# Rows turned by VectorE from 32-feature pieces, and one 512-column matmul for both parts of w2, in a two-layer mixture-of-experts kernel

## The chip, the cores and the metric

The kernel runs on one core of one Trainium2 chip. The metric is the device time of one execution in microseconds (us); lower is better. The median of three runs before the change is 2756.77 us (2755.84 to 2760.04).

## The reference

A Fourier transform over a batch of 8 x 3072 tokens of 256 features is followed by two mixture-of-experts layers, each with 8 experts of 256 -> 1024 -> 256 and one expert per token (top 1). Cut to what matters:

```python
def _attn_ref(x):                       # x: (8, 3072, 256)
    X = np.fft.fft(x, axis=1)
    X = np.fft.fft(X, axis=2)
    return X.real.astype(np.float32)

def _moe_ref(x, w_gate, w1, w2):        # x: (24576, 256)
    logits = x @ w_gate
    ...                                 # softmax, argmax
    for e in range(E):
        mask = expert_idx == e
        xe = x[mask]
        h = np.maximum(xe @ w1[e], 0.0)
        ye = h @ w2[e]
        out[mask] = gate_w[mask, None] * ye
```

The second layer (`_moe2_ref`) computes its logits from normalised rows and expert embeddings, and its experts in the same way.

## The kernel before, in words

The transform comes first (`fft`). Each of its rows is routed to an expert and scattered by GpSimd into a DRAM buffer `scr1`, grouped by expert: 256 features, the token's number and its gate, 258 floats a row (`ROWW`). Then follow two loops with the same code (`Layer.loop`): the first reads blocks of 256 rows (`T`) from `scr1`, computes the first layer's experts, routes again and scatters into `scr2`; the second reads `scr2` and scatters the results into `out`. Each loop runs some 99 steps, one block a step.

Precision: every factor of a matmul is split into a high and a low part in float32r, and the products high x high, high x low and low x high are summed in PSUM. So `x` becomes `xh` and `xl`, the hidden values `hh` and `hl`, the weights `w1h`, `w1l`, `w2h`, `w2l`.

A step `s` in the order in which it is written (and so stands in each engine's queue; `tc.manual_schedule()` keeps the written order):

- SyncE loads the block of step s + 2 (`load_rows`, L1179, one transfer into `xrow`; the first two blocks of a layer come earlier by `ahead`, L1186 and L1191), and, where the expert changes, the next weights into `stage` (L1042 to L1061). A step whose expert doesn't change skips those by a condition.
- `epilogue(s - 1)` begins: ScalarE evicts the accumulator `y` of the block before, times the gate, into `yrow` (`take`, L1273); in the first loop VectorE takes the eight logits (L1288), in the second the token numbers (L1278).
- `layer1`, four groups of 12 matmuls of 256 columns (L1243), each evicted by ScalarE (`hh`, relu, L1246) and VectorE (`hl`, relu and subtraction, L1247).
- `transpose` of the block s + 1 (L1228): TensorE turns the four 128 x 128 pieces into one PSUM bank `aux`, ScalarE casts `xh` (L1232), VectorE subtracts `xl` (L1233). `xh` and `xl` exist once, so this stands behind the step's first layer.
- the splitting of new weights, and in the first loop the routing on VectorE.
- `layer2` (L1255): 16 times (8 pieces of the hidden dimension, 2 halves of the block) three matmuls, hh x w2h, hh x w2l and hl x w2h, into `y[:, tb, :w2]`. In the first loop a row has 264 columns (256 and the 8 logits of the next router), in the second 256. `y` has one PSUM bank of 512 floats for each half.
- in the first loop TensorE counts ranks (L145, L148) from the one-hot `ohm` (L127); then GpSimd scatters (L178).

## Time and profile before

| | |
|---|---|
| median of 3 runs | 2756.77 us (2755.84 to 2760.04) |
| the profiled execution: time | 2754.11 us |
| the profiled execution: span of its instructions | 2752.2 us |
| TensorE matmul busy | 97% |
| VectorE, ScalarE, GpSimd busy | 47%, 39%, 29% |
| transform and routing ahead of the first loop | about the first 360 us |
| first loop, second loop | to about 1575 us, and from about 1600 to 2735 us |

A matmul's record runs from its start to the modelled end of its pipeline; the next one starts long before that end. So matmuls are priced by the distance from start to start, which the timeline gives, and the busy share says only that something was always under way.

### The profile page before, as it was taken

The numbers are of one execution on the slowest core, as the hardware profiler recorded it, in microseconds if no ns is written. First come the engines' busy times: TensorE is split into PE (matmuls) and PEld (weight loads), VectorE is DVE, ScalarE is ACT, GpSimd is POOL, SyncE is SP. The second block draws the span as 40 slices with busy tenths as digits, with TensorE's granted clock in tenths as the row PEclk, the third lists the DMA queues.
The fourth block names the chain that finished last, engine by engine and source line by source line (L and its number), as shares of the span: only waits on it lengthen the run. The fifth ranks groups of instructions, "written<-read, shape, count | busy, mean of one in ns | idle before, by whom it ended". The sixth has DMA issues, their size and how long they took to land. (4 is left out here: it accounts for less than half of the span.)

```text
span 2752.2 us, 66450 instructions
## 1 busy us (share of the span) xinstructions
PE 2659.2 (97%) x21695; PEld 2569.8 (93%) x21695; DVE 1306.1 (47%) x3870; ACT 1062.8 (39%) x2456; POOL 789.0 (29%) x875
## 2 busy tenths in 40 slices
PE   7888799999999999999999899999999999999998
PEld 4566689999999999999999899999999999999997
DVE  5776545556555665557555632343323323343232
ACT  2444434444444454445444433343333333343332
POOL 4877712233222332224222321111111111111111
PEclk9998899999999999999999999999999999999999
DMA  8677411122111331113111211131112211131121
GB/s 257 205 233 230 163 43 41 48 82 83 45 48 40 117 112 43 48 52 110 47 43 53 74 54 44 50 102 47 48 47 78 76 45 44 47 108 47 63 61 39
DMA packets 152349, 221.43 MB, mean 80 GB/s; under 512 B 40982, under 2 KB 120383, under 8 KB 151946
## 3 DMA queue, kind: packets, MB, share of 16 engines
q1 hardware_dynamic: 117658, 122.37, 16.3%
q0 software_dynamic: 31984, 94.02, 9.6%
q8 instruction: 180, 2.95, 0.5%
q14 instruction: 223, 1.83, 0.2%
q10 hardware_dynamic: 2304, 0.26, 0.1%
HBM read 529.18 MB, written 82.24 MB: 222 GB/s over the span
## 5 line engine op out<-in xcount | busy, mean ns | idle before, releaser
L1247 DVE SCALAR_TENSOR_TENSOR hl<-ph,hh 128x512 fp32r<-128x512 f32 x793 | 546.0, 691 | 904.2 <-ACT hh L1246 903.9
L1255 PE MATMUL py<-w2h,hh 128*128 128x264 f32 (+1 forms) x3184 | 918.1, 288 | 1.1 <-DVE lgm L1288 0.6
L1243 PE MATMUL ph<-xh,w1h 128*128 128x256 f32 x3172 | 900.4, 284 | 8.5 <-PEq L1485 5.5
L1255 PE MATMUL py<-w2h,hl 128*128 128x264 f32 (+1 forms) x3184 | 901.3, 283 | 0.1
L1255 PE MATMUL py<-w2l,hh 128*128 128x264 f32 (+1 forms) x3184 | 901.2, 283 | 0.2 <-DVE w2l L1097 0.2
L1243 PE MATMUL ph<-xh,w1l 128*128 128x256 f32 x3172 | 891.1, 281 | 0.0
L1243 PE MATMUL ph<-xl,w1h 128*128 128x256 f32 x3172 | 890.8, 281 | 0.1
L1246 ACT ACTIVATE hh<-ph 128x512 fp32r<-128x512 f32 x793 | 472.2, 599 | 574.6 <-PE ph L1243 562.1
L1243 PEld LDWEIGHTS ph<-xh,w1h 128*128 128x128 f32 x3172 | 599.5, 189 | 9.3 <-ACTq L1219 5.7
L1255 PEld LDWEIGHTS py<-w2h,hh 128*128 128x128 f32 x3184 | 601.4, 189 | 1.6 <-ACT hh L1246 1.5
L1255 PEld LDWEIGHTS py<-w2h,hl 128*128 128x128 f32 x3184 | 600.9, 189 | 0.9 <-DVE hl L1247 0.9
L1255 PEld LDWEIGHTS py<-w2l,hh 128*128 128x128 f32 x3184 | 601.4, 189 | 0.4 <-DVE w2l L1097 0.4
L1243 PEld LDWEIGHTS ph<-xh,w1l 128*128 128x128 f32 x3172 | 600.0, 189 | 0.0
L1243 PEld LDWEIGHTS ph<-xl,w1h 128*128 128x128 f32 x3172 | 599.6, 189 | 0.4 <-DVE xl L1233 0.4
L178 POOL DMA_INDIRECT out<-yrow,idx x194 | 188.7, 973 | 948.6 <-ACT yrow L1273 886.8
L1273 ACT ACTIVATE yrow<-py,xrow 128x256 f32<-128x256 f32 x368 | 154.4, 471 | 603.1 <-PE py L1255 431.9
L178 POOL DMA_INDIRECT scr<-yrow,pos x196 | 205.0, 1046 | 457.2 <-DVE lgm L1288 300.6
L178 POOL DMA_INDIRECT scr<-row,pos x192 | 208.0, 1084 | 69.8 <-issue 45.3
L1302 POOL TENSOR_TENSOR ssm<-ssm,half 128x2 f32<-128x2 f32 x98 | 75.1, 766 | 402.5 <-ACT sq L1299 379.4
L1233 DVE TENSOR_TENSOR xl<-aux,xh 128x512 fp32r<-128x512 f32 x201 | 136.9, 681 | 13.7 <-ACT xh L1232 7.7
L1232 ACT CAST xh<-aux 128x512 fp32r<-128x512 f32 x201 | 117.1, 582 | 18.2 <-PE aux L1228 18.2
L1228 PE MATMUL aux<-ident,xrow 128*128 128x128 f32 x736 | 110.3, 272 | 0.1
(276 smaller groups left out, 1925.1 us busy)
## 6 DMA issues: line engine op xcount, KB each, us to landing
stage<-in_moe_w SPq DMA_DIRECT2D x305, 1024.0 KB
stage<-in_moe_w SPq DMA_DIRECT2D x206, 512.0 KB
xrow<-scr SPq DMA_DIRECT2D x184, 258.0 KB
stage<-in_x SPq DMA_DIRECT2D x16, 768.0 KB
lw<-in_moe_w SPq DMA_DIRECT2D x8, 1024.0 KB
scr<-zrow SPq DMA_DIRECT2D x16, 258.0 KB
stage<-ext SPq DMA_DIRECT2D x102, 32.0 KB
scr<-yrow,pos POOLq DMA_INDIRECT x196, 3.3
```

The costliest lines, as they stand in the source:

```text
L178: ins = k.nc.gpsimd.indirect_dma_start(out=dst, out_offset=bass.IndirectOffsetOnAxis(ap=idx, axis=0), in_=src, in_offset=None, bounds_chec ...
L1228: nc.tensor.transpose(ps[:, dd * T + tb * P : dd * T + tb * P + P], t[:, tb, dd * P : dd * P + P], self.k.ident)
L1232: nc.scalar.copy(m.xh, pv)
L1233: self.v.tensor_tensor(m.xl, pv, m.xh, ALU.subtract)
L1243: nc.tensor.matmul(ps[:, f], lhsT=wa[i][:, dd, fs], rhs=xa[:, dd], start=n == 0, stop=n == 5)
L1246: nc.scalar.activation(m.hh[:, hs], ps, AF.Relu)
L1247: self.v.scalar_tensor_tensor(m.hl[:, hs], ps, 0.0, m.hh[:, hs], ALU.max, ALU.subtract)
L1255: self.nc.tensor.matmul(m.y[:, tb, : self.w2], lhsT=ha[:, f, ts_], rhs=wa[i][:, f, : self.w2], start=f == 0 and n == 0, stop=f == 7 and n ...
L1273: nc.scalar.activation(yr[:, tb, :D], y[:, tb, :D], AF.Copy, scale=tag[:, tb, 1:2])
L1302: nc.gpsimd.tensor_tensor(ss, ss, k.half, ALU.pow)
```

## The change

1. A block no longer comes as rows. `Rows` holds a tile `x` of 128 x 8 x 2 x 32 and a small tile `tag` with the token's number and gate. `fetch` loads `x` by four transfers, one for each quarter of the partitions, in pieces of 32 features (128 bytes), and `tag` by one.
2. `turn`, one VectorE instruction, transposes 32 x 32 blocks of `x` into `xt` (128 features x 2 x 256 tokens, SBUF). In the loops it stands between the beginning of the epilogue and the first layer. `parts` makes `xh` and `xl` from `xt` where `transpose` stood. The transposes on TensorE go.
3. The high and low parts of w2 lie beside each other in one tile (`w2hl`). In the second loop `layer2` makes one matmul of 512 columns, hh x (w2h | w2l), and one of 256 for hl x w2h. The two halves of the accumulator are added by VectorE in the epilogue, with the gate, onto `yrow`.
4. The pool `lt` (turned pieces of w2 ahead of the first loop) has three buffers instead of four.

```diff
+class Rows:
+    def __init__(self, pool, name, bufs=(1, 1)):
+        self.x = pool.tile([P, 8, 2, 32], F32, name=name + "x", bufs=bufs[0])
+        self.tag = pool.tile([P, 2, 2], F32, name=name + "t", bufs=bufs[1])
...
-    lo.wp = ctx.enter_context(tc.tile_pool(name="lt", bufs=4, side="right"))
+    lo.wp = ctx.enter_context(tc.tile_pool(name="lt", bufs=3, side="right"))
...
+            w = pool.tile([P, 8, 2, w2], F32R, name=f"w2{len(self.w2hl)}")
+            self.w2hl.append(w)
+            self.w2h.append(w[:, :, 0])
+            self.w2l.append(w[:, :, 1])
...
-            t = self.m.xr.tile([P, 2, ROWW], F32, name="xrow") if s < self.nlive else self.m.xe[s - self.nlive]
+            t = Rows(self.m.xr, "xrow", (4, 5)) if s < self.nlive else self.m.xe[s - self.nlive]
         r = self.reg(s, 0, 0, self.k.bound + 1 - T)
-        self.nc.sync.dma_start(t, self.src[ds(r, T)].rearrange("(a p) w -> p a w", p=P))
+        self.fetch(t, self.src[ds(r, T)])
         return t
+
+    def fetch(self, t, rows, tag=True, **kw):
+        v = rows[:, :D].rearrange("(j b) (a q i) -> q j b a i", b=8, a=2, q=4)
+        out = [self.nc.sync.dma_start(t.x[32 * q : 32 * q + 32], v[q], **kw) for q in range(4)]
+        if tag:
+            out.append(self.nc.sync.dma_start(t.tag, rows[:, D:ROWW].rearrange("(a p) w -> p a w", p=P), **kw))
+        return out
...
         for i in range(2):
-            ins = self.nc.sync.dma_start(
-                self.m.row[i], self.src[i * T : i * T + T].rearrange("(a p) w -> p a w", p=P), cond=(c != 0)
-            )
+            for ins in self.fetch(self.m.row[i], self.src[i * T : i * T + T], cond=(c != 0)):
...
-            self.nc.sync.dma_start(self.m.row[0][:, :, :D], other.rearrange("(a p) w -> p a w", p=P), cond=(c == 0))
+            self.fetch(self.m.row[0], other, False, cond=(c == 0))
...
+    def turn(self, t):
+        self.v.transpose(self.m.xt.rearrange("p a (j b) -> p b a j", b=8), t.x)
+
+    def parts(self):
+        m = self.m
+        self.nc.scalar.copy(m.xh, m.xt)
+        self.v.tensor_tensor(m.xl, m.xt, m.xh, ALU.subtract)
+
     def transpose(self, t):
-        nc, m = self.nc, self.m
-        ps = self.k.ps_aux.tile([P, 512], F32, name="aux")
-        for dd in range(2):
-            for tb in range(2):
-                nc.tensor.transpose(
-                    ps[:, dd * T + tb * P : dd * T + tb * P + P], t[:, tb, dd * P : dd * P + P], self.k.ident
-                )
-        pv = ps.rearrange("p (d t) -> p d t", d=2)
-        nc.scalar.copy(m.xh, pv)
-        self.v.tensor_tensor(m.xl, pv, m.xh, ALU.subtract)
+        self.turn(t)
+        self.parts()
...
+                first, last = f == 0, f == 7
+                if self.first:
...
+                else:
+                    nc.tensor.matmul(m.y[:, tb], lhsT=m.hh[:, f, ts_], rhs=m.w2hl[i][:, f, :, :D], start=first, stop=False)
+                    nc.tensor.matmul(m.y[:, tb, :D], lhsT=m.hl[:, f, ts_], rhs=m.w2h[i][:, f, :D], start=False, stop=last)
...
         if not self.first:
             take()
+            for tb in range(2):
+                v.scalar_tensor_tensor(yr[:, tb, :D], y[:, tb, D:], tag[:, tb, 1:2], yr[:, tb, :D], ALU.mult, ALU.add)
...
-            ep = self.epilogue(rows[s - 1][:, :, 256:258], s - 1)
+            ep = self.epilogue(rows[s - 1].tag, s - 1)
             next(ep)
...
+            if s + 1 < ns:
+                self.turn(rows[s + 1])
             for g in range(4):
                 self.layer1(s, g)
             if s + 1 < ns:
-                self.transpose(rows[s + 1])
+                self.parts()
```

Where the instructions stand is shown by three places. On TensorE, in a step of the second loop, from the last matmuls of the first layer to the first of the second, before:

```order
L1243 MATMUL ph<-xl,w1h_4421 128x256
L1243 MATMUL ph<-xh,w1l_4422 128x256
L1228 MATMUL aux<-ident,xrow 128x128 x4
L1255 MATMUL py<-w2h_4423,hh 128x256
L1255 MATMUL py<-w2l_4424,hh 128x256
L1255 MATMUL py<-w2h_4423,hl 128x256
```

and in the changed kernel (where w_4417 is the tile with both parts of w2):

```order
L1263 MATMUL ph<-xl,w1h_3426 128x256
L1263 MATMUL ph<-xh,w1l_3427 128x256
L1286 MATMUL py<-w_4417,hh 128x512
L1287 MATMUL py<-w_4417,hl 128x256
L1286 MATMUL py<-w_4417,hh 128x512
```

The four transposes are gone, and of three matmuls of 256 columns two have become one of 512.

On VectorE, in a step of the second loop, before (idx is the cast of the token numbers):

```order
L1278 CAST idx<-xrow 128x2
L1247 SCALAR_TENSOR_TENSOR hl<-ph,hh 128x512 x4
L1233 TENSOR_TENSOR xl<-aux,xh 128x512
L1172 TENSOR_LOAD bchange
L1219 COMPARE_AND_BRANCH
```

and in the changed kernel:

```order
L1304 SCALAR_TENSOR_TENSOR yrow<-py,xrowt,yrow 128x256 x2
L1306 CAST idx<-xrowt 128x2
L1244 STREAM_TRANSPOSE xt<-xrowx 128x8x64
L1267 SCALAR_TENSOR_TENSOR hl<-ph,hh 128x512 x4
L1249 TENSOR_TENSOR xl<-xt,xh 128x512
L1186 TENSOR_LOAD bchange
```

The two sums and the turn of the next block now stand ahead of the four `hl`; in the first loop it is the turn alone, behind the logits.

On SyncE, a row load of the second loop with the register loads around it, before:

```order
L1169 TENSOR_LOAD brow
L1169 ISA x2
L1179 ISA
L1179 DMA xrow<-scr_58 128x2x258
L1169 TENSOR_LOAD bchange
```

and in the changed kernel (each ISA row prepares the transfer behind it):

```order
L1198 ISA
L1198 DMA xrowx<-scr_58 32x16x32
L1198 ISA
L1198 DMA xrowx<-scr_58 32x16x32
L1198 ISA
L1198 DMA xrowx<-scr_58 32x16x32
L1200 ISA
L1200 DMA xrowt<-scr_58 128x2x2
L1183 TENSOR_LOAD bchange
```

One transfer has become five (the first of the four stands just above these rows), ahead of the conditional weight loads of the step.

## Rows read from the trace of the kernel before

**Rows 1.** The page: busy us by engine, and the clock in 40 slices

```profile
PE 2659.2 (97%) x21695; PEld 2569.8 (93%) x21695; DVE 1306.1 (47%) x3870; ACT 1062.8 (39%) x2456; POOL 789.0 (29%) x875
PEclk9998899999999999999999999999999999999999
```

**Rows 2.** Windows, first and second loop: stretch, length, busy by engine, clock, DMA share

```profile
360.00:1575.00 1215.00, 1201.21 (x10135) 1192.47 (x10134) 688.47 (x2501) 519.03 (x1232) 336.98 (x415) 0.99 0.22 63
1600.00:2735.00 1135.00, 1135.00 (x9664) 1135.00 (x9664) 375.12 (x610) 387.88 (x711) 188.69 (x194) 1.00 0.19 60
```

**Rows 3.** Timeline of TensorE, second loop: start, duration (us), line, operation

```profile
2004.81 0.28 PE L1243 MATMUL ph<-xh,w1l 128*128 128x256 f32 x1
...
2005.49 0.28 PE L1255 MATMUL py<-w2l,hh 128*128 128x256 f32 x1
...
2010.89 0.28 PE L1255 MATMUL py<-w2h,hl 128*128 128x256 f32 x1
2011.01 0.28 PE L1243 MATMUL ph<-xh,w1h 128*128 128x256 f32 x1
...
2016.55 0.28 PE L1243 MATMUL ph<-xh,w1l 128*128 128x256 f32 x1
2016.67 0.60 PE L1228 MATMUL aux<-ident,xrow 128*128 128x128 f32 x4
2017.02 0.36 PE L1255 MATMUL py<-w2h,hh 128*128 128x256 f32 x1
2017.22 0.28 PE L1255 MATMUL py<-w2l,hh 128*128 128x256 f32 x1
```

**Rows 4.** Line L1228 (count, ns min/median/max), and one group by form

```profile
L1228 PE MATMUL aux<-ident,xrow x736: 270/273/299, 386.1 to 2685.8; 128*128 128x128 f32 x184
L1228 PE MATMUL aux<-ident,row x48: 270/273/445, 314.1 to 2709.3; 128*128 128x128 f32 x48
L1228 PE MATMUL aux<-ident,xe x20: 271/273/273, 1530.0 to 2732.7; 128*128 128x128 f32 x20
...
L1255 PE MATMUL py<-w2l,hh 128*128 128x256 f32 x1584 | 444.9, 281 | 0.0
```

**Rows 5.** Timeline of the weight loads, ahead of the first loop

```profile
353.11 0.97 PEld L371 LDWEIGHTS aux<-en,wt 128*128 128x128 f32 x8
```

**Rows 6.** Timeline of VectorE, ScalarE and TensorE: a step of each loop

```profile
1016.42 0.17 DVE L1288 TENSOR_TENSOR lgm<-py,xrow 128x16 f32<-128x16 f32 x1 [0.63 <-DVEq L1214]
1017.09 0.69 DVE L1247 SCALAR_TENSOR_TENSOR hl<-ph,hh 128x512 fp32r<-128x512 f32 x1 [0.50 <-ACT hh L1246]
...
1020.89 0.37 PE L1255 MATMUL py<-w2h,hh 128*128 128x264 f32 x1
...
1023.89 0.17 DVE L127 TENSOR_TENSOR ohm<-eq,mx 128x16 f16<-128x16 f32 x1
...
1026.82 0.19 PE L145 MATMUL aux<-ohm,tri 128*128 128x24 f16 x1
...
2011.21 0.84 ACT L1273 ACTIVATE yrow<-py,xrow 128x256 f32<-128x256 f32 x2 [5.01 <-PE py L1255]
...
2013.26 0.69 DVE L1247 SCALAR_TENSOR_TENSOR hl<-ph,hh 128x512 fp32r<-128x512 f32 x1 [5.09 <-ACT hh L1246]
```

**Rows 7.** Groups by form: the weights' low part on VectorE

```profile
L1081 DVE TENSOR_TENSOR w1l<-stage,w1h 128x1024 fp32r<-128x1024 f32 x36 | 47.2, 1344 | 17.6 <-ACT w1h L1080 14.6 <-issue 1.7 <-DVEq L1214 1.2
```

**Rows 8.** DMA queues (packets, MB, share of 16 engines), and two issues on SyncE

```profile
q1 hardware_dynamic: 117658, 122.37, 16.3%
...
q10 hardware_dynamic: 2304, 0.26, 0.1%
...
44.51 12.41 SPq L485 DMA_DIRECT2D col<-in_x  x16
...
2009.81 0.38 SPq L1179 DMA_DIRECT2D xrow<-scr  x1
```

**Rows 9.** Timeline ahead of the first step (SyncE), and at the end (GpSimd)

```profile
310.74 1.12 SPq L1186 DMA_DIRECT2D row<-scr  x2
...
2741.29 0.97 POOL L178 DMA_INDIRECT out<-yf,idxf  x1 [11.31 <-ACT yf L1273]
```

More of the change, by code (lines that the diff above doesn't have):

```diff
@@ L1009, in __init__ @@
         self.k = k
-        self.w1h, self.w1l, self.w2h, self.w2l = [], [], [], []
+        self.w1h, self.w1l, self.w2hl, self.w2h, self.w2l = [], [], [], [], []
         self.st, self.st2, self.stx = zip(*(self.views(k, i) for i in range(2)))
     def add_set(self, pool, w2, parts=(1, 2)):
-        for part in parts:
-            hs, ls, shape = ((self.w1h, self.w1l, [P, 2, F]), (self.w2h, self.w2l, [P, 8, w2]))[part - 1]
-            for ws, n in ((hs, "h"), (ls, "l")):
-                ws.append(pool.tile(shape, F32R, name=f"w{part}{n}{len(ws)}"))
+        if 1 in parts:
+            for ws, n in ((self.w1h, "h"), (self.w1l, "l")):
+                ws.append(pool.tile([P, 2, F], F32R, name=f"w1{n}{len(ws)}"))
+        if 2 in parts:
+            w = pool.tile([P, 8, 2, w2], F32R, name=f"w2{len(self.w2hl)}")
+            self.w2hl.append(w)
+            self.w2h.append(w[:, :, 0])
+            self.w2l.append(w[:, :, 1])
     @staticmethod
@@ L1120, in open_rows @@
         self.xl = wp.tile([P, 2, T], F32R, name="xl")
-        self.row = [wp.tile([P, 2, ROWW], F32, name=f"row{i}") for i in range(4)]
+        self.xt = wp.tile([P, 2, T], F32, name="xt")
+        self.row = [Rows(wp, f"row{i}") for i in range(4)]
     def open_front(self, ctx):
@@ L1142, in open @@
         self.xr = ctx.enter_context(tc.tile_pool(name="mx", bufs=5))
-        self.xe = self.row[2:] + [wp.tile([P, 2, ROWW], F32, name=f"xe{i}") for i in range(E - 3)]
+        self.xe = self.row[2:] + [Rows(wp, f"xe{i}") for i in range(E - 3)]
         self.yp = ctx.enter_context(tc.tile_pool(name="my", bufs=3))
@@ L1159, in __init__ @@
         self.sets = m.sets
-        self.w2 = D + E if m.first else D
         self.nlive = self.k.nb * S // T
@@ L1185, in ahead @@
         for i in range(2):
[L1186 to L1189 removed]
+            for ins in self.fetch(self.m.row[i], self.src[i * T : i * T + T], cond=(c != 0)):
+                self.k.tc.add_to_no_dep_group("sc1" if self.first else "sc2", ins.ins if hasattr(ins, "ins") else ins)
         if other is not None:
[L1191 removed]
+            self.fetch(self.m.row[0], other, False, cond=(c == 0))
     def stage1(self, s):
@@ L1253, in layer2 @@
                 ts_ = slice(tb * P, tb * P + P)
-                for n, (ha, wa) in enumerate(((m.hh, m.w2h), (m.hh, m.w2l), (m.hl, m.w2h))):
-                    self.nc.tensor.matmul(
-                        m.y[:, tb, : self.w2],
-                        lhsT=ha[:, f, ts_],
-                        rhs=wa[i][:, f, : self.w2],
-                        start=f == 0 and n == 0,
-                        stop=f == 7 and n == 2,
-                    )
+                first, last = f == 0, f == 7
+                if self.first:
+                    for n, (ha, wa) in enumerate(((m.hh, m.w2h), (m.hh, m.w2l), (m.hl, m.w2h))):
+                        nc.tensor.matmul(
+                            m.y[:, tb, : D + E],
+                            lhsT=ha[:, f, ts_],
+                            rhs=wa[i][:, f, : D + E],
+                            start=first and n == 0,
+                            stop=last and n == 2,
+                        )
+                else:
+                    nc.tensor.matmul(m.y[:, tb], lhsT=m.hh[:, f, ts_], rhs=m.w2hl[i][:, f, :, :D], start=first, stop=False)
+                    nc.tensor.matmul(m.y[:, tb, :D], lhsT=m.hl[:, f, ts_], rhs=m.w2h[i][:, f, :D], start=False, stop=last)
     def epilogue(self, tag, s, edge=False):
@@ L1322, in early @@
             if s:
-                ep = self.epilogue(row[0][:, :, 256:258], 0, True)
+                ep = self.epilogue(row[0].tag, 0, True)
                 next(ep)
@@ L1356, in late @@
             if s == 0:
-                ep = self.epilogue(row[0][:, :, 256:258], 0, True)
+                ep = self.epilogue(row[0].tag, 0, True)
                 next(ep)
@@ L1384, in loop @@
                 Layer.ahead(self.after)
-            ep = self.epilogue(rows[s - 1][:, :, 256:258], s - 1)
+            ep = self.epilogue(rows[s - 1].tag, s - 1)
             next(ep)
             if s >= nlive - 1:
-                nc.scalar.copy(m.cur, rows[s][:, :, 256:258])
+                nc.scalar.copy(m.cur, rows[s].tag)
+            if s + 1 < ns:
+                self.turn(rows[s + 1])
             for g in range(4):
```

3 lines of the change are left out of this document (1 added, 2 removed).

## The prediction, made blind

> **What bounds the kernel now.** I read the page's busy times first: TensorE is busy 2659.2 of 2752.2 us and holds the upper clock level (2.4 GHz) in nearly all slices [rows 1]. A share over the whole span says little, so next came the stretches: TensorE is busy 1201.21 of 1215 us in the first loop and 1135.00 of 1135 us in the second, while VectorE is busy 57% and 33%, and the DMA engines 22% and 19% [rows 2]. So in both loops TensorE's instruction stream sets the time, and the reader is to see what one step of it is made of.
>
> The timeline of one step of the second loop shows that [rows 3]. A busy time of 0.28 us for one matmul is not its price: the next starts 0.117 us later. From 2005.49 to 2010.89 lie 46 starts, so 5.40 / 46 = 0.1174 us. Going from the second layer's matmuls to the first layer's costs nothing extra (2010.89 to 2011.01). Going the other way, four transposes stand between, and there lies 2016.55 to 2017.22 = 0.67 us where two plain spacings would be 0.235 us: the four transposes and the slow first matmul behind them cost **0.44 us a step**. A step is 2016.55 - 2004.81 = 11.74 us (the same place one step earlier [rows 3]), so this is 3.7% of it.
>
> **The change, part by part.** *Transposes leave TensorE.* There are 736 + 48 + 20 = 804 of them [rows 4], 201 groups of four; each saves 0.44 us where TensorE runs without idling: 201 x 0.44 = 88 us. That holds only if what takes their place is hidden.
>
> *VectorE turns the rows.* No row shows such an instruction. It moves 512 columns from SBUF to SBUF; the nearest row is the weights' remainder, 1,024 columns SBUF to SBUF in 1.344 us [rows 7], so I take half, 0.67 us, with ends 0.5 (no fixed part) and 1.34 (each element passes twice). It stands ahead of the four hl instructions of its step. First loop: lgm ends at 1016.59, hl starts at 1017.09 because it waits for ScalarE [rows 6]; the turn fills that gap and delays the first hl by 0.2 to 0.85 us, to an end of 1018.6 at most. TensorE wants it at 1020.89. The later hl's each wait some 0.7 us for ScalarE, so the delay is gone by the second or third, and the one-hot ohm behind them (1023.89, wanted by TensorE at 1026.82) stays. Cost: 0, hidden behind the first layer's 5.6 us of matmuls.
>
> *The sum on VectorE in the second loop.* Two instructions of 256 columns; the same operation of 512 columns takes 0.69 us [rows 6], so at most 0.69 each. They wait for ScalarE's two evictions (2011.21 + 0.84 = 2012.05 [rows 6]). Queued behind them: the cast, the turn, the hl's. At the upper ends: 2012.05 + 1.4 + 0.2 + 1.34 = 2015.0, first hl done by 2015.7 instead of 2013.95; TensorE wants it at about 2017. Cost 0, with 1.3 us in hand. The accumulator y is read out by 2013.5, before it is written again at 2017. GpSimd's scatter waits about 1 us longer, and nothing waits for that but the end of the program.
>
> *xh and xl* read SBUF instead of PSUM, at the same place behind the last matmul of the first layer; some 5 us of second layer cover them. I take 0.
>
> *Row loads.* One transfer of 256 pieces becomes four of 512 pieces of 128 bytes and one of 256 pieces of 8. SyncE: sixteen transfers of 128 x 6 single floats, 768 pieces each, were issued in 12.41 us [rows 8], 0.78 us each or 1.0 ns a piece, so 2,304 pieces are about 2.3 us of issue for 0.38 now. Moved past that are only the weight loads of later steps, in a queue that waits for VectorE anyway. On the engines the nearest row by size is q10: 2,304 packets of 113 bytes on average in 0.1% of 16 x 2752 us, 19 ns each (10 to 29 by rounding); the other end is q1, 1,040 bytes on average, 16.3% over 117,658 packets, 61 ns [rows 8]. A row load is then 2304 x 19 / 16 = 2.7 us of every engine (8.8 at 61 ns). The load issued at 2009.81 [rows 8] belongs to the block that is turned at the start of the step after next, about 2024.7: 15 us of lead against 2.3 + 2.7 (11.1 at the upper end). Hidden.
>
> The Trainium skill speaks against this part ("DMA: Bandwidth & Descriptors", Specifications: transfers want pieces of at least 512 bytes for full rate, below that the engines read, modify and write). The trace agrees in bytes: 113 bytes in 19 ns is a third of the rate of 1,040 in 61. It changes the sum only if the row loads become the bound, which is the third rival.
>
> *One matmul of 512 columns for two of 256.* There are 1,584 such pairs [rows 4]. Two now cost 0.235 us. The one cannot be below 512 columns / 2.4 GHz = 0.213 us, and not above 0.235, since the same columns pass with one weight load less: a saving of 0 to 22 ns a pair, 0 to 34 us. What decides is whether the 0.117 - 0.107 = 10.7 ns that a 256-column matmul takes beyond its columns come per instruction or per column. Eight weight loads beside 8-column matmuls span 0.97 us, (0.97 - 0.19) / 7 = 0.111 us each [rows 5]: weights alone come nearly as slowly as the matmuls do, so the surplus looks tied to the load, one per instruction. I take 10.7 ns saved: 1584 x 0.0107 = **17 us**.
>
> By the Trainium skill ("TensorE: Matmul & The Clock Gate", Back-to-back issue gap) a matmul costs its columns plus about 2.5 ns. No row of the two loops agrees, 256 columns take 10.7 more; yet where 512 columns hide the load, that page's 0.216 us would save 19 ns a pair, 30 us, which is the first rival.
>
> *The ends.* Ahead of the first step SyncE issues two row loads in 1.12 us [rows 9]; now ten transfers and four more, and the turn of the first block stands in VectorE's queue ahead of weights and logits: 0 to 8 us once, and a little again between the layers; I take 4. At the end the sum adds at most 1.4 us ahead of the last scatter (2741.29 [rows 9]): 1. The smaller buffer count of the pool lt I price at 0: its next writer stands behind its last reader in TensorE's order already.
>
> **Sum**, against the profiled execution's own 2754.1 us (its span of 2752.2 and 1.9 around it): 2754.1 - 88 - 17 + 5 = 2654. The median of the three runs is 2.7 us above that execution, so 2657.
>
> **Rivals.** *First: a 512-column matmul at the bare column rate* (no surplus, since the load is long done): 30 to 34 us in place of 17, so 2640 to 2644. For it speaks the 0.111 us weight load; against it, that it needs the surplus to vanish whole.
>
> *Second: the surplus goes with the columns* (reading the moving operand is a little slower than the clock). Then the merge saves nothing and only the transposes count: 2757 - 88 + 5 = 2674. Nothing in the rows excludes it, since all matmuls of the loops have about one width.
>
> *Third, on the other side: the small pieces make the DMA engines the bound.* A step then lasts as long as its transfers: about 20% of 11.74 us are taken already, 2.3 us, and 144 pieces an engine come on top. From (11.74 - 2.3) / 144 = 66 ns a piece the step is longer than today, and the turn in VectorE's queue holds hl and with it TensorE. At 75 ns: 13.1 us a step, 1.4 x 198 steps = 277 us more, about 3030. For it: unaligned 128-byte reads from HBM beside weights, which no row shows; against it: q10's 10 to 29 ns, and col's pieces went by at 16 x 1.0 = 16 ns an engine.
>
> *Fourth: VectorE late in part.* If the turn costs 3 to 5 us, the first hl in the first loop comes after 1020.89, and ohm late: 0.4 us or more of 100 steps returns, 2700 to 2760. Against it: no row of 512 columns is above 0.7 us.
>
> That the transposes don't really go can be left aside: they are gone from TensorE's order.
>
> **How the numbers follow.** Forecast 2657: 0.55. First rival 0.16, second 0.16, third 0.07, fourth 0.06. The unknown ends (0 to 10 us) widen the three lower cases to 2636 to 2685; that holds 0.87, and the range ends there. A difference of 0.2% (5.5 us) is about what a measurement of this kernel can tell from no change. The first three cases are all faster, 0.87, and of the fourth I count 0.02 faster, 0.03 the same and 0.01 slower; with the third rival that makes 0.89, 0.03 and 0.08.
>
> **What would show it.** The matmuls of the two loops keep a spacing of 0.117 us, and a step of the second loop falls from 11.74 to 11.74 - 0.44 - 16 x 0.0107 = 11.13 us, of the first by 0.44. The 512-column matmul's start to the next start reads 0.213 to 0.235: that settles the first two rivals. VectorE's wait at the turn should be on y's eviction or nothing, not on a DMA; if a DMA ends it, the third rival is at work. The first hl should come by 2 us after where it is now at most, with no wait of TensorE for hl. The prediction is wrong if TensorE idles in the loops, or if the spacing of the 256-column matmuls grows because VectorE and the transfers now move more through SBUF.

## The result, and the profile after

The changed kernel takes 2698.28 us (median of four runs, 2691.82 to 2700.54), the kernel before, run beside it, 2758.4 us (2755.84 to 2760.32): a ratio of 0.9779, with an interval of 0.9765 to 0.9794. So it is faster, as forecast, but by 60 us where the forecast had 100, and it lies outside the range of 2636 to 2685. On a second chip the same two kernels gave 2699.54 and 2759.36 us, 0.9785 (0.9767 to 0.9804).

The page of the changed kernel (busy time by engine, the clock in 40 slices, the queue that carries the row loads) answers to [rows 1] and [rows 8], two of its windows (stretch, length, busy by engine, clock, DMA share) to [rows 2]:

```profile
PE 2574.2 (95%) x19307; PEld 2411.2 (89%) x19307; DVE 1575.5 (58%) x4269; ACT 1069.6 (40%) x2456; POOL 791.9 (29%) x875
...
PEclk9898789999999999999999999999999999999999
...
q1 hardware_dynamic: 546394, 122.42, 23.4%
```

```profile
400.00:1480.00 1080.00, 1067.37 (x8968) 1059.59 (x8967) 721.75 (x2399) 477.32 (x1123) 309.21 (x382) 0.99 0.30 65
1560.00:2680.00 1120.00, 1114.13 (x7901) 1041.27 (x7902) 559.62 (x961) 403.14 (x735) 198.96 (x202) 1.00 0.28 61
```

TensorE still has work in nearly all of both loops, and the DMA engines rose from 0.22 and 0.19 to 0.30 and 0.28 of their time without becoming the bound. What the windows hide is seen only when the steps are lined up one by one. The table is worked out from the start of the first matmul of each step (L1243 before, L1263 after), span against span:

| stretch | before, us | after, us | difference | the forecast's |
|---|---|---|---|---|
| start of the program to the first step | 315.4 | 327.4 | +12.0 | +4 |
| the first four steps | 78.1 | 82.1 | +4.0 | -1.8 |
| 87 steps of the first loop with no change of weights | 1054.6 | 1016.2 | -38.4 | -38.3 |
| the 7 steps that bring in an expert's new weights | 90.1 | 106.1 | +15.9 | -3.1 |
| step 94 of the first loop | 12.1 | 13.3 | +1.2 | -0.4 |
| the 4 steps between the loops | 61.8 | 58.9 | -2.9 | -2 |
| the 95 remaining steps of the second loop | 1114.7 | 1068.8 | -45.9 | -58.1 |
| behind the last step's start | 25.4 | 25.1 | -0.3 | +1 |
| span | 2752.2 | 2697.8 | -54.4 | -99 |

Three lines are wrong: the ends (with the first four steps, some 14 us), the weight-change steps (19 us, and 1.6 us in step 94) and the second loop (12 us). The expectations below count eight weight-change steps. The eighth is step 94 (steps count from 0): in it no weights are combined or split, and it grew for another reason, shown further down. The sums over eight steps are kept, so that they can be held against the expectations.

The second loop first. The timeline of TensorE there (start, duration in us, line, operation; it answers to [rows 3]):

```profile
2003.17 0.28 PE L1263 MATMUL ph<-xh,w1l 128*128 128x256 f32 x1
2003.28 0.40 PE L1286 MATMUL py<-w,hh 128*128 128x512 f32 x1
2003.52 0.28 PE L1287 MATMUL py<-w,hl 128*128 128x256 f32 x1
2003.64 0.39 PE L1286 MATMUL py<-w,hh 128*128 128x512 f32 x1
...
2008.88 0.29 PE L1263 MATMUL ph<-xh,w1h 128*128 128x256 f32 x1
...
2014.43 0.28 PE L1263 MATMUL ph<-xh,w1l 128*128 128x256 f32 x1
...
2020.18 0.28 PE L1263 MATMUL ph<-xh,w1h 128*128 128x256 f32 x1
```

The transposes are gone: from the last matmul of the first layer to the first of the second it is 0.11 us, one plain spacing. A step takes 2014.43 - 2003.17 = 11.26 us. But the 512-column matmul starts 0.24 us before the next one and its 256-column neighbour 0.12: sixteen pairs fill 2008.88 - 2003.28 = 5.60 us, 0.350 us a pair, where three matmuls of 256 columns took 3 x 0.117 = 0.352.

Now a weight-change step of the first loop. The same step before and after, from the timelines of GpSimd, VectorE and TensorE (in brackets the idle time of the engine just ahead, and what ended it). Before:

```profile
611.66 0.36 PE L1243 MATMUL ph<-xh,w1h 128*128 128x256 f32 x1
...
617.31 0.17 DVE L1288 TENSOR_TENSOR lgm<-py,xrow 128x16 f32<-128x16 f32 x1
617.39 2.48 DVE L1247 SCALAR_TENSOR_TENSOR hl<-ph,hh 128x512 fp32r<-128x512 f32 x4
...
617.35 0.60 PE L1228 MATMUL aux<-ident,xrow 128*128 128x128 f32 x4
617.70 0.37 PE L1255 MATMUL py<-w2h,hh 128*128 128x264 f32 x1
```

After:

```profile
617.21 4.75 POOL L1084 TENSOR_TENSOR stage<-stage 127x1024 f32<-127x1024 f32 x2
...
617.58 2.06 DVE L142 TENSOR_TENSOR dl<-dl,ssm 128x16 f32<-128x16 f32 x1
...
623.37 2.36 DVE L1095 TENSOR_TENSOR w1l<-stage,w1h 128x1024 fp32r<-128x1024 f32 x2 [0.43 <-ACT w1h L1094]
625.65 0.17 DVE L1316 TENSOR_TENSOR lgm<-py,xrowt 128x16 f32<-128x16 f32 x1
625.74 1.11 DVE L1244 STREAM_TRANSPOSE xt<-xrowx 128x512 f32<-128x512 f32 x1
626.70 2.46 DVE L1267 SCALAR_TENSOR_TENSOR hl<-ph,hh 128x512 fp32r<-128x512 f32 x4
...
619.59 0.36 PE L1263 MATMUL ph<-xh,w1h 128*128 128x256 f32 x1
625.96 0.48 PE L1277 MATMUL py<-w,hh 128*128 128x264 f32 x2 [0.53 <-DVE lgm L1316]
627.42 0.39 PE L1277 MATMUL py<-w,hl 128*128 128x264 f32 x1 [0.98 <-DVE hl L1267]
```

In such a step GpSimd combines two raw weights (L1084), ScalarE and VectorE split them (L1095), and only then does VectorE read the logits lgm, which frees the accumulator that the second layer wants. Before, lgm was done at 617.48 and the first hl at 617.39 + 0.69 = 618.08; the four transposes lay on TensorE at just that moment, the second layer began behind them at 617.70, and hardly anything waited. After, this chain is no shorter, but the step in which it begins is, by 0.44 us: lgm comes 6.06 us after the step's first matmul instead of 5.65, TensorE wants it 0.44 us sooner, and between lgm and the first hl stands the turn. TensorE waits twice, 0.53 and 0.98 us by the rows.

In some of these steps the waits cost a second time. The windows of the next weight-change step, 656.82 to 672.10 in the same trace:

```profile
656.80:662.40 5.60, 5.60 (x51) 5.60 (x51) 4.70 (x11) 4.35 (x8) 3.80 (x3) 1.00 0.58 146
662.40:664.90 2.50, 0.97 (x7) 0.58 (x6) 2.50 (x5) 1.38 (x3) 1.43 (x2) 1.00 0.62 213
664.90:668.00 3.10, 3.10 (x15) 3.10 (x16) 3.10 (x5) 3.06 (x7) 0.00 (x0) 0.50 0.44 72
668.00:672.00 4.00, 4.00 (x33) 3.95 (x32) 3.41 (x17) 0.22 (x2) 1.33 (x2) 0.96 0.21 27
```

TensorE was busy for 0.97 of 2.5 us there, and in the 3.1 us behind that its granted clock reads 0.50, the lower of its two levels (1.2 of 2.4 GHz): 15 matmuls where some 26 would go. This step took 15.27 us (12.88 before); the one shown above it, whose clock did not fall, took 13.89 (12.60 before).

The small VectorE instruction L142, shown above, took 2.06 us beside GpSimd's L1084; the median of its 98 is 0.17 us. The Trainium skill has a rule for this ("GPSIMD Engine Reference", Specifications: GpSimd's way to SBUF is shared with VectorE instructions that read two SBUF tensors or run in a two-port mode), and the row agrees. Before the change GpSimd's combinations held up small VectorE instructions as well, though mostly others: twelve of them by 1.6 to 2.2 us each, 21.5 us in the first loop, where it is 24.6 after. So this is part of why VectorE is late in these steps in both kernels, and little of the difference.

Step 94 grew by a late row load. SyncE's issues and the turn (start, duration, what ended the wait):

```profile
1464.60 3.34 SPq L1198 DMA_DIRECT2D row0x<-scr  x4
...
1468.97 3.30 SPq L1198 DMA_DIRECT2D row1x<-scr  x4
...
1479.04 3.00 SPq L1198 DMA_DIRECT2D xrowx<-scr  x4
...
1484.95 1.11 DVE L1244 STREAM_TRANSPOSE xt<-xrowx 128x512 f32<-128x512 f32 x1 [4.01 <-DMA xrowx<-scr]
```

The loads of the second loop's first two blocks stand ahead of it in SyncE's queue, ten transfers where there were two, and the turn waits 4.01 us. The turn waited for its rows in three more steps of the first loop (1.21, 2.73 and 1.43 us in steps 3, 50 and 56). Step 50 lost some 0.4 us by it, step 56 nothing.

Last, the front, with SyncE's issues, the first turn and the first matmul of the first step:

```profile
315.18 3.48 SPq L1198 DMA_DIRECT2D row0x<-scr  x4
...
319.73 3.29 SPq L1198 DMA_DIRECT2D row1x<-scr  x4
...
324.00 1.52 SPq L1198 DMA_DIRECT2D row0x<-in_x  x4
...
325.52 1.10 DVE L1244 STREAM_TRANSPOSE xt<-row0x 128x512 f32<-128x512 f32 x1 [7.16 <-DMA row0x<-in_x]
...
327.42 0.55 PE L1263 MATMUL pss<-xh,w1h 128*128 128x256 f32 x1 [9.07 <-issue]
```

Each small-piece transfer holds SyncE for 0.8 us, and the turn of row0 waits for the very last, behind the load of row1. From the flag (the VectorE instruction whose result picks the loads; L906 before, L915 after) to the first step it is 327.42 - 309.87 = 17.6 us, before 315.44 - 305.54 = 9.9. Other runs have 9.0 and 13.3 us with the old front (e6, e5) and 16.8 to 18.3 with the new one (a0, e8, e11, e12), so the new front costs some 3 to 9 us. The other 4.3 us of the 12.0 lie ahead of the flag, in the transform, and move from run to run: with the old front the flag also stood at 313.0 and 311.1 us (the kernels e5 and e6 below), with the new one also at 306.0 (e12).

### The profile page after: what moved, and what is told of

Same layout as the page of the kernel before. It is cut to its first block, busy times and chain, and to the rows that moved or that the text cites. A ratio compares the mean times of both kernels' runs of the same rounds, so it can differ in the third digit from the quotient of the medians.

```text
span 2697.8 us, 64848 instructions
## 1 busy us (share of the span) xinstructions
PE 2574.2 (95%) x19307; PEld 2411.2 (89%) x19307; DVE 1575.5 (58%) x4269; ACT 1069.6 (40%) x2456; POOL 791.9 (29%) x875
## 3 DMA queue, kind: packets, MB, share of 16 engines
q1 hardware_dynamic: 546394, 122.42, 23.4%
## 5 line engine op out<-in xcount | busy, mean ns | idle before, releaser
L1263 PE MATMUL ph<-xh,w1h 128*128 128x256 f32 x3172 | 899.0, 283 | 12.2 <-ACT xh L1248 6.9
L1263 PE MATMUL ph<-xl,w1h 128*128 128x256 f32 x3172 | 890.0, 281 | 0.5 <-DVE xl L1249 0.3
L1263 PE MATMUL ph<-xh,w1l 128*128 128x256 f32 x3172 | 890.2, 281 | 0.0
L1263 PEld LDWEIGHTS ph<-xh,w1h 128*128 128x128 f32 x3172 | 598.3, 189 | 17.3 <-ACT xh L1248 7.5
L1277 PE MATMUL py<-w,hh 128*128 128x264 f32 x3200 | 600.0, 287 | 9.7 <-DVE lgm L1316 4.4
L1263 PEld LDWEIGHTS ph<-xl,w1h 128*128 128x128 f32 x3172 | 599.5, 189 | 1.0 <-DVE xl L1249 1.0
L1263 PEld LDWEIGHTS ph<-xh,w1l 128*128 128x128 f32 x3172 | 598.9, 189 | 0.2 <-DVEq L1233 0.2
L1286 PE MATMUL py<-w,hh 128*128 128x512 f32 x1584 | 560.8, 396 | 0.0
L1277 PEld LDWEIGHTS py<-w,hh 128*128 128x128 f32 x3200 | 502.8, 191 | 11.3 <-ACT hh L1266 9.9
L1277 PE MATMUL py<-w,hl 128*128 128x264 f32 x1600 | 460.3, 288 | 10.3 <-DVE hl L1267 10.3
L1287 PE MATMUL py<-w,hl 128*128 128x256 f32 x1584 | 443.9, 280 | 0.0
L1299 ACT ACTIVATE yrow<-py,xrowt 128x256 f32<-128x256 f32 x368 | 154.7, 472 | 523.4 <-PE py L1287 384.6
L1286 PEld LDWEIGHTS py<-w,hh 128*128 128x128 f32 x1584 | 297.1, 188 | 67.8
L1277 PEld LDWEIGHTS py<-w,hl 128*128 128x128 f32 x1600 | 305.4, 191 | 12.5 <-DVE hl L1267 12.5
L1304 DVE SCALAR_TENSOR_TENSOR yrow<-py,xrowt,yrow 128x256 f32<-128x256 f32 x184 | 80.5, 479 | 382.3 <-ACT yrow L1299 382.3
L1287 PEld LDWEIGHTS py<-w,hl 128*128 128x128 f32 x1584 | 298.5, 188 | 0.0
L1244 DVE STREAM_TRANSPOSE xt<-xrowx 128x512 f32<-128x512 f32 x184 | 220.1, 1196 | 12.7 <-DMA xrowx<-scr 10.0
```

The costliest lines, as they stand in the source:

```text
L1244: self.v.transpose(self.m.xt.rearrange("p a (j b) -> p b a j", b=8), t.x)
L1263: nc.tensor.matmul(ps[:, f], lhsT=wa[i][:, dd, fs], rhs=xa[:, dd], start=n == 0, stop=n == 5)
L1277: nc.tensor.matmul(m.y[:, tb, : D + E], lhsT=ha[:, f, ts_], rhs=wa[i][:, f, : D + E], start=first and n == 0, stop=last and n == 2,)
L1286: nc.tensor.matmul(m.y[:, tb], lhsT=m.hh[:, f, ts_], rhs=m.w2hl[i][:, f, :, :D], start=first, stop=False)
L1287: nc.tensor.matmul(m.y[:, tb, :D], lhsT=m.hl[:, f, ts_], rhs=m.w2h[i][:, f, :D], start=False, stop=last)
L1299: nc.scalar.activation(yr[:, tb, :D], y[:, tb, :D], AF.Copy, scale=tag[:, tb, 1:2])
```

## Experiments

Some of the chips took some 40 to 60 us longer in the transform than others (e1 to e4 and e13), so their times are compared with the kernel before on the same chip, and stages are compared by the trace: there the plain steps of the loops agree between chips. The eight steps do not: in seven traces whose first loop is the changed kernel's (it twice, e1, e4, e11, e12, e13) they take 116.5 to 127.2 us, and in three that are as before there (the kernel before, e2, e5) 102.2 to 104.8. A difference of a few us between two traces says nothing there by itself.

**e1: the merge undone.** Second loop with three matmuls of 256 columns, no sum.

```
-nc.tensor.matmul(m.y[:, tb], lhsT=m.hh[:, f, ts_], rhs=m.w2hl[i][:, f, :, :D], ...)
-nc.tensor.matmul(m.y[:, tb, :D], lhsT=m.hl[:, f, ts_], rhs=m.w2h[i][:, f, :D], ...)
+for n, (ha, wa) in enumerate(((m.hh, m.w2h), (m.hh, m.w2l), (m.hl, m.w2h))):
+    nc.tensor.matmul(m.y[:, tb, :D], lhsT=ha[:, f, ts_], rhs=wa[i][:, f, :D], ...)
```

> The changed kernel with one part undone: in the second loop three matmuls of 256 columns again, and no sum on VectorE. Theory (what a matmul takes beyond its columns at 2.4 GHz goes with the columns, so the merge gave 2.6 ns a pair): 4 us slower than the changed kernel, 2702, steps of the second loop 11.24 us instead of 11.20, all spacings 0.117 us. Forecast's step (10.7 ns a pair, tied to the weight load): 17 us slower, 2715. If the sum on VectorE cost something, it would be faster than 2698.

Ratio to the kernel before 0.9808 (0.9746 to 0.9869); the whole can't tell 5 us on that chip, the stage can. The 95 steps of the second loop take 1073.8 us instead of 1068.8 (1068.8 in every other trace with these pairs and this order): the merge is worth 5.0 us there, 3.3 ns a pair and not 10.7.

**e2: the merge alone**, on the kernel before.

> The kernel before with the merge alone: 512-column matmuls and the sum on VectorE in the second loop, the rows transposed by TensorE from plain transfers. Theory (2.6 ns a pair): 2754, 4 us below the kernel before. Forecast's step (10.7 ns a pair): 2741. A rival, that the 512-column matmul is only slow in the changed kernel because small transfers and the turn disturb it: its spacing would read under 0.225 us here, and the time 2741 or less.

0.9996 (0.9966 to 1.0025); the 95 steps take 1111.8 us instead of 1114.7, 1.9 ns a pair. The rival falls: the wide matmul is as slow without the turn and the small transfers (0.234 us to the next start by the median, as in the changed kernel).

**e3: the turn behind the four hl.** This was to free hl.

```
-if s + 1 < ns:
-    self.turn(rows[s + 1])
 for g in range(4):
     self.layer1(s, g)
 if s + 1 < ns:
+    self.turn(rows[s + 1])
     self.parts()
```

> The changed kernel with the turn moved behind the four hl of its step, just ahead of xl, in both loops. Theory (the turn, 1.1 us, stands in VectorE's queue ahead of hl, and in the steps that change weights in the first loop VectorE is already late there, partly because the turn waits for its row transfer): the eight weight-change steps of the first loop lose the 20 us that they cost, 2698 - 20 = 2678, some 2 us more if step 3 mends too. Rival (those steps are late because of the weight loads behind the small transfers on SyncE, or because the DMA engines are fuller): they stay, 2694 to 2700.

Both missed: 0.9894 (0.9845 to 0.9943), where e1 and e4 on that chip have 0.9808 and 0.9829. The intervals overlap, the stages don't: the eight steps take 138.8 us (e1 120.7, e4 127.2), the 87 plain ones 1022.2 instead of 1016. The waits of TensorE (us in total, times, longest), the changed kernel's first:

```profile
PE py L1277 <- DVE hl L1267: 10.3, 10, 2.0
...
PE py L1277 <- DVE lgm L1316: 4.4, 6, 1.7
```

```profile
PE py L1277 <- DVE lgm L1316: 18.3, 6, 3.6
...
PE aux L154 <- DVE ohm L136: 15.4, 17, 2.4
```

The wait for hl is gone (0.2 us), as meant, but the turn now stands ahead of xh, and behind xh on ScalarE stand the squares that GpSimd's power waits for, behind which it combines the next weights. So the turn delayed the chain squares, combination, w1l, lgm, which the theory had not seen. The trace has it: in the first weight-change step the squares begin 2.1 us ahead of the step's first matmul instead of 4.4 (e4), the combination 0.1 us behind it instead of 2.2 ahead, and lgm 8.5 us behind it instead of 6.3.

**e4: the first block's loads ahead of the second's.**

```
 for i in range(2):
     for ins in self.fetch(self.m.row[i], ...): ...
-if other is not None:
-    self.fetch(self.m.row[0], other, False, cond=(c == 0))
+    if i == 0 and other is not None:
+        self.fetch(self.m.row[0], other, False, cond=(c == 0))
```

> The changed kernel with one order changed at the front: SyncE issues the second conditional load of the first block (row0 from the input) ahead of the load of the second block (row1) instead of behind it. Theory (the first turn waits for SyncE's issue of fourteen transfers, 315.2 to 325.5 us): the turn starts about 4 us earlier, at 321.5, and the whole is 4 us shorter, 2694. Rival (the first step waits for something else by then, weights or logits): the first step starts less than 1 us earlier and the time stays 2698.

0.9829 (0.9795 to 0.9863). The whole can't tell 4 us there, the stage can: from the flag to the first step 28.0 us, against 33.3 and 32.1 in e1 and e3 on that chip, and the turn no longer waits for a transfer. The kernel e2, with the old front, has 28.2 us there.

**The changed kernel once more, and e8: the turn behind the first hl.**

> The changed kernel once more, so that the next three have it beside them on the same chip. Expected: 0.978 of the kernel before; the eight weight-change steps of the first loop 14 to 17.5 us each, regular steps 11.63 and 11.72 us, TensorE waiting some 10 us for hl and 4 us for lgm.

```
 for g in range(4):
     self.layer1(s, g)
+    if g == 0 and s + 1 < ns:
+        self.turn(rows[s + 1])
```

> The changed kernel with the turn between the first hl and the other three of its step. Theory: in a weight-change step VectorE comes late to lgm, and the turn of 1.1 us stands between lgm and the first hl, for which TensorE waits; behind the first hl it is hidden (TensorE needs the second hl 2.9 us after the first), and it is done before xh and the norms, which start the chain to GpSimd's combination of weights that a turn behind all four hl delayed. So TensorE's waits for hl go (10 us to under 2), waits for lgm stay near 4, and the eight steps lose 9 to 12 us: 2698 - 11 = 2687. Rival (GpSimd's combination and the two w1l instructions set the end of those steps whatever the turn does): the wait moves from hl to lgm and the time stays within 3 us of the changed kernel.

The changed kernel: 2699.54 us (2698.17 to 2702.06), eight steps 120.0, waits for hl 11.8 and for lgm 5.7 us. e8: 2692.17 us (2690.87 to 2696.09; 0.9758, 0.9740 to 0.9777), eight steps 115.2 (1.9 of these 4.8 us in step 94). The waits of e8:

```profile
PE aux L154 <- DVE ohm L136: 11.3, 8, 4.0
...
PE py L1277 <- DVE lgm L1316: 3.5, 5, 1.4
PE py L1277 <- DVE hl L1267: 0.3, 1, 0.3
```

hl is cured and lgm stays, as the theory had it, but the gain of 9 to 12 us in these steps did not come; the wait moved: VectorE is still late in these steps, and now TensorE meets it at the one-hot ohm, which stands in VectorE's queue behind xl and the splits of w2 (2.4 us in the first loop of the changed kernel on that chip). The rival had a wait that moves, though to the wrong place.

**e9: e8 and e4 together.**

> The turn behind the first hl, and at the front the load of row0 from the input ahead of row1. Theory: the two gains add, 11 + 4: 2683, and from the flag to the first step it takes 4 to 5 us less than in the changed kernel. Rival: they overlap nowhere, so only either gain alone not being real would give another time.

2688.70 us (0.9745, 0.9727 to 0.9764), 3.5 us below e8, less than the whole can tell; from the flag to the first step 14.7 us where the changed kernel on that chip has 16.8. That is 2 us of the 4 to 5 expected: the first turn still waits 4.3 us for its rows there.

**e10: the squares and the router's first steps ahead of xh and xl**, on e9.

```
+next(ep)
 if s + 1 < ns:
     self.parts()
 self.split2(s + 1)
 self.stage2(s + 2)
-next(ep)
```

> As the one before, and the two squares (and the router's first VectorE steps) of a step ahead of xh and xl on ScalarE and VectorE. Theory (the chain squares, GpSimd's power, GpSimd's combination, w1l, lgm sets the weight-change steps once the turn is out of the way): GpSimd starts the combination 0.6 to 0.7 us earlier, and eight steps lose 0.5 us each: 4 us less than the one before, 2679. Rival (the combination waits for its transfers, or xl comes too late for the next step): no gain, or regular steps above 11.72 us.

2680.25 us (0.9714, 0.9695 to 0.9733), 8.4 us below e9 and twice the expected gain, for another reason than the expected one: waits for lgm stayed (4.5 us), those for ohm fell from 10.5 to 1.3 us, since the one-hot now stands ahead of xl and the w2 splits. The squares begin 0.7 us earlier but the combination does not: GpSimd waits 1.18 us for the weights' transfer there in the first weight-change step, as the rival had it. The eight steps take 104.6 us, inside the 102.2 to 104.8 of the traces that are as before there.

**e5 and e6: the two suspects apart**, each added to the kernel before, writing to a spare tile.

```
+for q in range(4):
+    self.nc.sync.dma_start(xs[32 * q : 32 * q + 32], v[q])
```

> The kernel before, and behind each row load of the two loops the four small-piece transfers of the same rows into a spare tile that nothing reads. Theory (the pieces hide in the loops: 3 us of SyncE's issue and 2 to 3 us of each DMA engine in a step of 12): within 4 us of the kernel before, 2758 to 2762, the eight weight-change steps of the first loop 102 to 105 us in all as before. Rival (weights come late behind the pieces on SyncE, which is what lengthened those steps in the changed kernel): 2.5 us more in each of them, 122 us in all, 2778.

```
+x = rows[s + 1][:, :, :D].rearrange("p a (b i) -> p b a i", b=8)
+v.transpose(m.yf[:, :, :D].rearrange("p a (j b) -> p b a j", b=8), x)
```

> The kernel before, and one turn of a row block into a spare tile that nothing reads, where the changed kernel has it (ahead of the four hl of each step in both loops). Theory (the turn's place on VectorE is what lengthened the weight-change steps): regular steps stay 12.08 and 12.16, 11.69 and 11.77 us, the eight weight-change steps gain 1.1 to 2.1 us each, 102 + 13 = 115 us in all, the time 2758 + 13 = 2771. Rival (the pieces did it): the eight steps within 3 us of 102, the time within 4 us of the kernel before.

e5: 1.0005 (0.9995 to 1.0014), eight steps 103.6 us. The small pieces slow nothing else in the loops; but nothing waits for them here, so a turn that waits for late rows, as in step 94, is not tested by it. e6: 1.0032 (1.0019 to 1.0045), eight steps 108.4 us, the plain ones unchanged. So the turn's place costs 4 to 6 us of its own in these steps. TensorE waits there for hl (6.6 us), and hardly for lgm (0.4 us), since the transposes still stand ahead of the matmul that wants it; without them, in the changed kernel, it waits 4.4 us for lgm as well. The other 14 us of the forecast's error in these steps come when the transposes go: the steps then don't shorten with them (3 us), TensorE arrives sooner at a VectorE that is no sooner, and the clock falls behind some of the longer waits (in four of the steps 13 to 18 matmuls follow 0.22 us apart, 0.1 us more than elsewhere: some 5 us). Step 94 has 1.6 us of them. How the rest divides was not measured part by part.

**e11 to e14: why the merge gives so little.**

> The changed kernel, with the 512-column matmul of the second loop fed 2-byte operands: the upper halves of hh as weights, and as moving side a constant tile read twice instead of w2's two parts (so this product is left out of the result). Theory (the 4-byte moving side passes a little slower than the clock, whatever the width): its start to the next start falls from 0.234 to 0.216 us or less, and a step of the second loop by 16 x 0.018 = 0.3 us, to 10.9. Rival (the surplus is PSUM's, 512 single floats written by one matmul, or a fixed part of every matmul): it stays at 0.23, steps 11.2 us.

The pair still takes 0.35 us (wide matmuls start at 2004.55, 2004.90, 2005.25), so the theory's gain did not come. The start of the wide one to that of the narrow one, which was to be read, is no measure here: it reads 0.04 us, and the rest 0.31. Nor can this run rule out that a change between 2-byte and 4-byte matmuls has a price of its own that eats the gain. Measured alone, behind the program's last matmul:

> The changed kernel with 320 matmuls more behind its last one, in groups of 40 that nothing reads: 512, 384, 256 and 128 columns of 4-byte operands, then 512 and 256 columns of 2-byte operands, once with 2-byte weights that lie together and once with every second half of 4-byte ones. Read is the start to the next start in a group. Theory A (what a matmul takes beyond its columns at 2.4 GHz goes with the columns, whatever the operands): 234, 176, 117 and, unless the weight load of 111 ns holds it, 59 ns; 2-byte ones 234 and 117 too. Theory B (it is the 4-byte moving side): the 2-byte groups 213 to 216 and 107 to 109 ns. Theory C, the forecast's (about 11 ns for each matmul, with its weight load): 224, 171, 117, 64 or 111 ns. The wide matmuls of the loops measured 232 to 234 ns, which speaks against C.

The timeline of TensorE in the middle of six groups of e12, in order (the duration is that of all xN together):

```profile
2685.84 1.98 PE L1546 MATMUL py<-w1h,hh 128*128 128x512 f32 x8
...
2694.69 2.07 PE L1546 MATMUL py<-w1h,hh 128*128 128x384 f32 x11
...
2700.80 1.96 PE L1546 MATMUL py<-w1h,hh 128*128 128x256 f32 x15
...
2705.78 1.95 PE L1546 MATMUL py<-w1h,hh 128*128 128x128 f32 x16
...
2711.83 1.89 PE L1552 MATMUL py<-wb 128*128 128x512 bf16 x8
...
2718.75 1.47 PE L1552 MATMUL py<-wb 128*128 128x256 bf16 x12
```

From start to start, averaged over the 39 distances of each group: 4-byte operands 229, 174, 119.7 and 110 ns for 512, 384, 256 and 128 columns (median 227, 173, 120, 111), 2-byte ones 216 and 109. So among equal neighbours a 4-byte matmul takes its columns at 2.4 GHz and about 13 ns, whatever its width, until at 128 columns the distance is that of the weight loads, 111 ns [rows 5]. The 4-byte figures are nearest to theory C's, the 2-byte ones are theory B's: the surplus comes per matmul, and with 4-byte operands. Two 256-column matmuls merged would save 2 x 119.7 - 227 = 12 ns. The forecast's reason was right for that, and the loop is not like that.

The Trainium skill ("TensorE: Matmul & The Clock Gate", Back-to-back issue gap) gives, for a matmul by itself, the columns at 2.4 GHz and 2.5 ns. The 2-byte groups agree (213.3 + 2.5 = 215.8, 216 measured; 109.2, 109 measured), the 4-byte groups don't.

> The changed kernel with groups of matmuls more behind its last one, that nothing reads. Three groups of 48 pairs (512 columns, then 256 with other weights into the same accumulator, as in the second loop): accumulating, each overwriting, and accumulating with the loop's own w2 as the moving side. Then 48 matmuls each: 512 columns accumulating over two banks, over one bank, overwriting one bank; 256 accumulating over one bank, over two. Theory A (the other engines' work on SBUF and PSUM in the loop slows the wide matmul): all pairs take 227 + 120 = 347 ns or less here, against 351 in the loop. Theory B (accumulation into the bank just written): accumulating pairs 351, overwriting ones 347; 512 columns over one bank 234, over two 227. Theory C (the pair itself, two kinds of weights): 351 in all three groups, and 227 in all groups of 512.

With the other engines idle the pairs take 353 ns accumulating (without the first one, 424), 353 overwriting and 350 with the loop's own w2, the groups of 512 columns 227 ns each way, those of 256 columns 120. Pairs of e13, then a group of equal ones:

```profile
2786.56 0.40 PE L1547 MATMUL py<-w1h,hh 128*128 128x512 f32 x1
2786.79 0.28 PE L1548 MATMUL py<-w1h,hl 128*128 128x256 f32 x1
2786.91 0.40 PE L1547 MATMUL py<-w1h,hh 128*128 128x512 f32 x1
...
2835.79 1.98 PE L1559 MATMUL py<-w1h,hh 128*128 128x512 f32 x8
```

Theory C holds: it is the pair itself (350 to 353 where equal neighbours would give 347). Neither the other engines' traffic nor accumulation does it.

> The kernel of e10, and in both loops the second layer's products with hl behind all those with hh of the same two feature blocks: in the second loop four matmuls of 512 columns, then four of 256, in place of four pairs. Theory (the change of width between neighbours eats the gain of the merge): four pairs take 4 x (227 + 120) = 1387 ns where they took 1405, a step of the second loop 11.18 us instead of 11.25, 7 us in all; and hl, wanted 0.5 us later, is waited for even less: 2680 - 8 = 2672. Rival (a wide matmul beside narrow ones in the same stream costs 234 ns wherever it stands): steps of the second loop stay 11.20 and 11.30 us, 2678 to 2682.

In words, on e10:

```
-for f, tb: hh x w2 (512 columns), hl x w2h (256 columns)
+for f, tb: hh x w2 (512 columns)
+for f, tb: hl x w2h (256 columns)
```

2677.51 us (0.9703, 0.9683 to 0.9723). The 95 steps of the second loop take 1066.4 instead of 1068.8 us, a third of what the theory had, and four wide matmuls in a row stand 0.231 us apart, between the 0.234 of the pairs and the 0.227 of a long row: the rival is nearer. The loop is not needed for that. In e13 the row of 512 columns behind the last pairs begins with 230, 236, 229 and 232 ns, and keeps to 227 only from the sixth on, and e12's rows of 512 and 384 columns settle in the same way. So what the wide matmul loses goes with the change of width among its neighbours; why stays open. Waits for hl are gone, but the 87 plain steps of the first loop grew by 2.2 us. e10 and e14 beat both kernels, by the ratios to the kernel before, and can't be told apart from each other.

## Why the forecast was right, and where it was wrong

- *What bounds the kernel, and the transposes.* Right for the plain steps: the 87 of the first loop lost 0.44 us each, those of the second 0.43 to 0.45 (from the kernel before to e1, and from e2 to the changed kernel). Wrong to count on it in every one of the 201 groups: in the seven weight-change steps and in step 3 TensorE only came sooner to a wait.
- *The merge, 17 us.* Wrong; in 95 steps it gave 2.9 us (e2) to 5.0 (e1), 1.9 to 3.3 ns a pair. The failed step is "I take 10.7 ns saved". It rested on weight loads at 0.111 us [rows 5], read as a surplus that goes with each instruction. e12 shows that saving, 12 ns, between equal neighbours; the pair of a wide and a narrow matmul doesn't give it (e13), since the wide one takes 234 ns there instead of 227, and the narrow ones that it replaced stood 118 ns apart (e1), not 119.7. The first rival is out: 0.234 us, not 0.216. The second rival, "the merge saves nothing", describes the result, by another cause than the one it named. Its end of 0 had rightly been kept for the range.
- *The turn, "Cost: 0".* Wrong in the seven weight-change steps, and right in the plain ones of both loops. The instruction takes 1.196 us on average, inside the ends of 0.5 to 1.34 but near the upper one. The step that failed is older: the working took a plain step [rows 6] and read off that lgm, hl and ohm have room. In the steps that bring new weights VectorE has none. It was late there already, and the transposes on TensorE covered that; without them TensorE waited 10.3 us for hl and 4.4 for lgm in the run, and the steps grew by 15.9 us where they were to shrink by 3. The page's average hides these steps, and so does a single timeline. The fourth rival had the mechanism, but asked for a turn of 3 to 5 us and put it in every step.
- *The sum, xh and xl: 0.* Right. The sum's two instructions take 0.48 us each, behind ScalarE's evictions, and in the second loop TensorE waits for nothing.
- *Row loads, hidden.* Right for nearly all steps, although a load holds SyncE for 3.7 us (median) and not 2.3. Wrong in step 94, and in part in step 3, which grew by 5.8 us. There GpSimd, which starts behind the transform's scatters, begins the power behind its squares at the same time after the first step as before (67.9 us, 67.7 before) while TensorE comes 1.9 us sooner, and TensorE's wait for hh is 3.42 us instead of 0.51. Then SyncE issues the four pieces from 395.27 to 398.33, the turn waits 1.21 us for them and TensorE 1.96 us for hl, and the clock falls for 6.8 us (granted clock 0.50). So the sign that was named for the third rival, a DMA that ends the turn's wait, did come, in four steps of the first loop (9.4 us in all), without the rival: the DMA engines' share rose (0.22 to 0.30) and did not become the bound. The queue moved the same 122.4 MB in 23.4% of the engines' span instead of 16.3%, which agrees with the rule of the Trainium skill on pieces under 512 bytes ("DMA: Bandwidth & Descriptors", Specifications).
- *The ends, 5.* Too low: flag to first step 7.7 us instead of 4 in this pair of traces, because the first turn waits for all fourteen issues (e4 and e9 give 2 to 5 of that back); and between the layers step 94 lost 1.6 us by the same kind of wait.
- *The range.* It held the unknown merge and ends, but left VectorE late in part outside, as the fourth rival with 0.06. By the spans the error is 45 us: 12 in the second loop, 19 in the seven weight-change steps, 2 in step 94, 14 at the front and in the first four steps, and 2 back elsewhere. The medians lie 41 us from the forecast.

## What to carry to other kernels

Before you take work off the bounding engine, look for what that work covers: an engine that is late by just its length shows no wait in the profile, and waits as soon as it is gone. Price an added instruction in the steps where its queue is fullest (here the seven of a hundred that change weights), not in the typical one, and follow the queue behind it to whoever waits last, since a wait that is removed at hl comes back at ohm. When an instruction has three places to stand, try them: the turn cost most behind the last hl, where it was to free hl.

## What the runs showed of the hardware

- A 4-byte matmul of 256 to 512 columns among equal ones takes some 13 ns beyond its columns at 2.4 GHz, a 2-byte one 2.5 (e12); a 512-column one beside a 256-column one takes 234 to 236 ns instead of 227, also with nothing else at work (e13).
- VectorE's turn of 128 x 512 single floats takes 1.09 to 1.26 us (201 in the changed kernel).
- A transfer of 512 pieces of 128 bytes holds SyncE for 0.78 us (median, start to next start), and for up to 2.6 us in the slowest cases.
- Behind a stretch in which TensorE was busy 0.97 of 2.5 us, its granted clock read 0.50 for 3.1 us. In the weight-change step ahead of it, with nearly the same gaps between starts (0.81 and 1.26 us; 0.82 and 1.27 where the clock fell), the matmuls behind them kept their spacing.
- A small VectorE instruction of 0.17 us took 2.06 us beside a GpSimd operation on 127 x 1024 single floats.
